# Attention, Fourier mixer and gated mixer on one core: residual additions by accumulating transfers in a rewritten order

## Chip, core and metric

One core of a Trainium2 chip runs the kernel; the other cores are empty. The metric is the device time of one execution in microseconds (us). Below, TensorE is the matrix engine (PE in the profile, PEld its weight loads), VectorE is DVE, ScalarE is ACT, GpSimd is POOL, SyncE is SP. SBUF is the on-chip memory of 128 partitions, PSUM the accumulator memory of eight banks that only TensorE's products, VectorE and ScalarE reach.

## The reference, cut to what matters

```python
# attention: q, k, v are (4 batches, 4 heads, 1088, 32); S1, S2 are (8, 32)
phi(x)  = (x @ S1.T)[..., :, None] * (x @ S2.T)[..., None, :]     # 64 features
kv      = phi(k).T @ v ;  z = phi(k).sum(over the sequence)
x       = (phi(q) @ kv) / (phi(q) @ z + 1e-6)                     # heads joined: (4, 1088, 128)
# first mixture
u       = x + real(fft(fft(x, axis=sequence), axis=channels))
un      = (u - mean(u)) / sqrt(var(u) + 1e-6)
y       = u + relu(un @ w_ch1) @ w_ch2                            # 128 -> 512 -> 128
# second mixture
h       = relu(y @ w_in)                                          # 128 -> 1024
conv    = 3 taps along the sequence, weights per channel
out     = (h * sigmoid(conv)) @ w_out                             # 1024 -> 128
```

All in float32.

## The kernel before

**Layout.** Channels (or features) lie on the 128 partitions and the sequence of 1088 along the free axis. Four batches go through the same stages: `load_attn`, `attn`, `fft`, `moe1`, `moe2`. A batch's sequence is cut into three pieces of 364, 364 and 360 columns (`PIECES`) wherever it goes through PSUM.

**Precision.** A product with plain float32 operands takes two records in the trace. Where speed matters an operand is split into two parts of type float32r, a rounded `hi` and the rest `lo` (`lo_of`: one VectorE operation), and three products replace one: hi·hi, lo·hi, hi·lo. So `z<-yh,win_hi`, `z<-yh,win_lo` and `z<-yl,win_hi` in the trace belong together.

**attn(b)** (lines 309 to 449). `kab_ps` are the two projections of k, `kp` their outer products (VectorE), `kv_ps` the sums over the sequence. In batches 0, 1 and 3 `kv_ps` is transposed by one more product into `kvt_ps`. Four small copies by VectorE then bring it to SBUF: per half of the partitions `kv` (64x64) and `zz` (64x2, `z` in the trace). `den` needs `zz`, `num` needs `kv`. q's features `qa` come in batch 0 from products with repeated weights (`qab_ps`, 128x364); in batches 1 to 3 from small products (`qab_ps`, 128x273), a copy by ScalarE to `qab`, a round trip through DRAM (`qd`) and a product on VectorE. `qab` has a buffer of its own in the pool `at`. The attention output is `x`.

**fft(b)** (from line 452). `xe`, `xo` and `parts` are sums and differences on VectorE; `p_ps` the channel transform, `spec` four sums over the sequence (even and odd frequencies, each an even part `e_ps` and an odd part `o_ps`, 272 columns). For each parity VectorE forms `osb = o_ps - x` and `u = e_ps - osb` for one half of the sequence and `osb = o_ps + x`, `u = e_ps + osb` for the mirrored half, and one column more for the even parity: eight operations of 272 columns and one of one column.

**moe1(b)** (from line 506). ScalarE copies `u` to `uh`, VectorE forms `ul`; products `z` (with `w1`) and `cen` follow, `hid` is the relu. `norm` gives `y`, the reciprocal deviation spread over the partitions. `down(i)` sums `ch` in PSUM, and VectorE multiplies by `y` and adds `u`, both in PSUM; ScalarE copies the result to `yh`, VectorE forms `yl`.

**moe2(b)** (from line 587). Eight chunks of 128 channels: products `z` and relu `h` (ScalarE), middle tap `t` (ScalarE), two outer taps (VectorE, 1087 columns), sigmoid (ScalarE), product with `h` (VectorE), and `acc`, three banks that sum over the chunks.

**Start.** `load64` brings weights as 64-bit words and decodes them with six VectorE operations each 512 columns. `idle` are products of a zero tile `still` with itself whose result nobody reads; 24 of them.

**Buffers.** `slot` gives a tile of the shared wide pool (`mo=12` buffers). PSUM has five banks `mm` and three banks `acc`.

**Order.** Nothing runs as the functions are called: `Program` records 1,956 operations, and `issue` (line 153) sends them in the order of the list `ORDER`, written out as numbers. Every engine's queue is thus a cut of that list, each engine works its own queue in order, and waits follow from the data. In it work of one batch stands between that of the next. All operations are issued by one helper, line 157, which is why the profile puts them on that line; the names of tiles tell them apart. DMAs stand on SP's queue, in the list's order as well; GpSimd issues three loads at the start and makes four broadcasts for batch 0.

Of the kernel before, what the change touches and what calls it, by code (L numbers as in the profile page):

```python
# [19 lines left out]
P = dict(near=(0,), kvt=(0, 1, 3), hs=(), hlo=4, xb=2, sq=(0,), rpe=(0,), up=(0,), mo=12, hid=7, idle=24)  # L20
# [4 lines left out]
D = 128  # L25
# [135 lines left out]
def tile_fwd(ctx, tc, qT, kT, va, srep, mats, thi, tlo, tend, w1, w2, win, cw, wout, out):  # L161
# [73 lines left out]
    if P["idle"]:  # L235

        idle = bank("idle", "acc")
        for i in range(P["idle"]):
            T.matmul(idle[:, :128], still[:, :128], still[:, 128:], start=True, stop=True)
# [494 lines left out]
```

## Time and profile before

| | |
|---|---|
| median of 3 runs | 260.95 us (260.68 to 262.37) |
| profiled execution | 261.13 us |
| its span, first to last instruction | 259.4 us |
| mean granted TensorE clock | 0.993 of full speed |
| instructions | 4622 |
| HBM read, written | 23.27 MB, 3.31 MB |

The profile is of one execution. Matmul records are pipelined and overlap, so an engine that is busy all the time need not be at its peak; what two products cost one behind the other is read from the spacing of their starts, which the chain of waits shows. A granted clock of 1.00 is 2.4 GHz and 0.50 is 1.2 GHz.

### The profile page before, as it was taken

The numbers are of one execution on the slowest core, as the hardware profiler recorded it, in microseconds if no ns is written. First come the engines' busy times: TensorE is split into PE (matmuls) and PEld (weight loads), VectorE is DVE, ScalarE is ACT, GpSimd is POOL, SyncE is SP. The second block draws the span as 40 slices with busy tenths as digits, with TensorE's granted clock in tenths as the row PEclk, the third lists the DMA queues.
The fourth block names the chain that finished last, engine by engine and source line by source line (L and its number), as shares of the span: only waits on it lengthen the run. The fifth ranks groups of instructions, "written<-read, shape, count | busy, mean of one in ns | idle before, by whom it ended". The sixth has DMA issues, their size and how long they took to land.

```text
span 259.4 us, 4622 instructions
## 1 busy us (share of the span) xinstructions
PE 250.8 (97%) x1812; PEld 198.5 (77%) x1812; DVE 234.4 (90%) x356; ACT 183.6 (71%) x330; POOL 6.5 (2%) x15
## 2 busy tenths in 40 slices
PE   7799999999999999999989999999999999999994
PEld 7566679876979887778878877678988877877652
DVE  2588999988999999989999999999999998999970
ACT  3342433972986847873788978996999998999822
POOL 1400000030000000000000000000000000000000
PEclk9799999999999999999999999999999999999999
DMA  7999299385568204184303001500000050000202
GB/s 225 329 402 284 85 304 236 115 228 179 123 147 195 75 24 122 42 175 131 86 4 114 11 0 15 137 0 0 3 0 29 9 143 0 0 3 1 85 0 86
DMA packets 11557, 26.87 MB, mean 104 GB/s; under 512 B 2224, under 2 KB 6832, under 8 KB 11280
## 3 DMA queue, kind: packets, MB, share of 16 engines
q1 hardware_dynamic: 11136, 23.92, 32.9%
q0 software_dynamic: 400, 2.67, 2.9%
q8 instruction: 14, 0.23, 0.4%
q14 instruction: 7, 0.06, 0.1%
HBM read 23.27 MB, written 3.31 MB: 102 GB/s over the span
## 4 chain that ended last, share of the span: by engine, by line
PE 81%; DVE 10%; DMA 4%; ACT 2%; issue 1%; SPq 0%; ACTq 0%; DVEq 0%
PE z L157 25%; PE acc L157 20%; PE ch L157 10%; PE qab_ps L157 5%; DMA q<-qT 4%; PE spec L157 4%; PE kv_ps L157 4%; DVE t L157 4%; PE p_ps L157 3%; PE num L157 3%; PE kab_ps L157 2%; PE cen L157 2%; ACT t L157 1%; PE var L157 1%; DVE ch L157 1%
## 5 line engine op out<-in xcount | busy, mean ns | idle before, releaser
L157 DVE SCALAR_TENSOR_TENSOR t<-h,cw_sb,t 128x1087 f32<-128x1087 f32 x64 | 83.8, 1340 | 0.9 <-ACT t L157 0.4
L157 PE MATMUL acc<-t,wo_sb 128*128 128x364 f32 (+1 forms) x192 | 69.3, 469 | 0.0
L157 ACT ACTIVATE h<-z 128x364 f32<-128x364 f32 (+1 forms) x96 | 41.0, 472 | 15.2 <-PE z L157 14.8
L157 DVE TENSOR_TENSOR t<-t,h 128x1088 f32<-128x1088 f32 (+2 forms) x34 | 40.9, 1217 | 4.6 <-ACT t L157 4.5
L157 PEld LDWEIGHTS acc<-t,wo_sb 128*128 128x128 f32 x192 | 34.3, 189 | 9.1 <-DVE t L157 0.6
L157 ACT ACTIVATE t<-h,cw_sb 128x1088 f32<-128x1088 f32 x32 | 38.4, 1204 | 0.4
L157 ACT ACTIVATE t<-t 128x1088 f32<-128x1088 f32 (+2 forms) x34 | 35.5, 1058 | 4.3 <-DVE t L157 4.3
L157 PE MATMUL z<-yh,win_hi 128*128 128x364 f32 (+1 forms) x96 | 37.2, 414 | 0.0
L157 PE MATMUL z<-yl,win_hi 128*128 128x364 f32 (+1 forms) x96 | 34.1, 366 | 0.2 <-DVE yl L157 0.2
L157 PE MATMUL z<-yh,win_lo 128*128 128x364 f32 (+1 forms) x96 | 34.1, 359 | 0.0
L157 PE MATMUL ch<-hid,w_sb 128*128 128x364 f32 (+1 forms) x96 | 33.3, 469 | 0.0
L157 ACT ACTIVATE hid<-z 128x364 f32<-128x364 f32 (+1 forms) x48 | 21.3, 474 | 7.4 <-PE z L157 7.1
L157 PEld LDWEIGHTS ch<-hid,w_sb 128*128 128x128 f32 x96 | 17.3, 189 | 6.6 <-ACT hid L157 0.5
L157 PEld LDWEIGHTS z<-yh,win_hi 128*128 128x128 f32 x96 | 17.7, 189 | 5.1 <-ACT h L157 1.0
L157 PEld LDWEIGHTS z<-yh,win_lo 128*128 128x128 f32 x96 | 18.1, 189 | 3.1
L157 PEld LDWEIGHTS z<-yl,win_hi 128*128 128x128 f32 x96 | 18.0, 189 | 2.6 <-DVE yl L157 0.5
L157 PE MATMUL z<-uh,w_hi 128*128 128x364 f32 (+1 forms) x48 | 19.2, 410 | 0.0
L157 PE MATMUL z<-uh,w_lo 128*128 128x364 f32 (+1 forms) x48 | 16.9, 358 | 0.0
L157 PE MATMUL z<-ul,w_hi 128*128 128x364 f32 (+1 forms) x48 | 16.4, 359 | 0.0
L157 PE MATMUL p_ps<-mats_sb,parts 128*32 128x128 f32 (+1 forms) x160 | 15.4, 276 | 0.7 <-ACT pe L157 0.7
L157 PEld LDWEIGHTS p_ps<-mats_sb,parts 128*32 128x32 f32 (+1 forms) x160 | 13.2, 142 | 2.2 <-ACT pe L157 0.9
L157 DVE TENSOR_TENSOR kp<-kab_ps,kb 121x512 f32<-121x512 f32 (+1 forms) x24 | 12.2, 546 | 0.5 <-ACT kb L157 0.5
(118 smaller groups left out, 389.3 us busy)
## 6 DMA issues: line engine op xcount, KB each, us to landing
qa<-qd SPq DMA_DIRECT2D x6, 546.0 KB
qb<-qd SPq DMA_DIRECT2D x12, 273.0 KB
v<-va SPq DMA_DIRECT2D x4, 594.0 KB
q<-qT SPq DMA_DIRECT2D x4, 546.0 KB, 6.4
k<-kT SPq DMA_DIRECT2D x4, 544.5 KB
x<-rrd SPq DMA_DIRECT2D x12, 136.5 KB, 4.1
y<-rtd SPq DMA_DIRECT2D x3, 544.0 KB
out<-r SPq DMA_DIRECT2D x8, 182.0 KB
```

The source lines that it names most:

```text
L157: fn(*args, **kw)
```

## The change

- `idle`: 36 products instead of 24; `still` has 128 columns and is both operands.
- `kva`: in batches 0 and 1 ScalarE makes the four copies to `kv` and `zz`.
- `ua`: in batches 1 to 3 ScalarE copies `o_ps` to `osb` and the one column to `u`; VectorE forms `u = e_ps ∓ osb` (four operations of 272 columns); then one transfer issued by GpSimd, from SBUF to SBUF, adds `x` onto `u` (128x1088).
- `ca`: in batch 2 VectorE writes `ch * y` over `y` in SBUF, and per piece a transfer issued by GpSimd adds `u` onto it; `yh` and `yl` are made from there.
- `qab` takes a slot of the wide pool.
- `load64` writes the decoded value into its place one operation earlier; the operations are as many.
- `dm`, `dl`, `ea` and `hs` are empty in this kernel, so what hangs on them isn't built.
- `ORDER` is new: 1,965 numbers, all positions changed. In the new list 17 idle products stand ahead of TensorE's first product on q (13 before); the load of q for batch 2 stands ahead of the transfers of `qd`; and TensorE's queue has, between the last `spec` product of a batch and the first product on its `uh`, in batch 1 17 z, 8 acc and 7 kab products (16 z and 4 acc before), in batch 2 33 and 9 (7 and 4), in batch 3 26 and 9 (15 and 4), z counted in records of three to a product and acc in products. Between the last `ch` product of a piece of batch 2 and the first z on its `yh` stand 6.5, 7.2 and 5.8 us of products for the first, middle and last piece by the durations of the trace.

```diff
-P = dict(near=(0,), kvt=(0, 1, 3), hs=(), hlo=4, xb=2, sq=(0,), rpe=(0,), up=(0,), mo=12, hid=7, idle=24)
+P = dict(near=(0,), kvt=(0, 1, 3), hs=(), hlo=4, xb=2, sq=(0,), rpe=(0,), up=(0,), mo=12, hid=7, dm=(), dl=(), late=2, kva=(0, 1), ua=(1, 2, 3), ca=(2,), ea=(), idle=36)
...
-            V.scalar_tensor_tensor(ei, hi, -(1 << 30), ei, op0=ALU.bitwise_and, op1=ALU.bitwise_or)
-            V.tensor_scalar(mi, ei, -(1 << 23), None, op0=ALU.bitwise_and)
+            x = use(o, w, e)
+            xi = x.bitcast(I32)
+            V.scalar_tensor_tensor(xi, hi, -(1 << 30), ei, op0=ALU.bitwise_and, op1=ALU.bitwise_or)
+            V.tensor_scalar(mi, xi, -(1 << 23), None, op0=ALU.bitwise_and)
...
-    still = cst.tile([128, 256], F32, name="still")
+    still = cst.tile([128, 128], F32, name="still")
...
-            T.matmul(idle[:, :128], still[:, :128], still[:, 128:], start=True, stop=True)
+            T.matmul(idle[:, :128], still, still, start=True, stop=True)
...
-            qab = at.tile([128, SP // 2], F32, tag="qab", name=f"qab{b}")
+            qab = slot(f"qab{b}")[:, :SP // 2]
...
-            V.tensor_copy(kv[r, :, 32 * h2:32 * h2 + 32], kvv[h2][:, :, 0:32])
-            V.tensor_copy(zz[r, DJ - 1 + DJ * h2:DJ + DJ * h2 + ZW + 2 * DJ:ZW + 2 * DJ], kvv[h2][:, :, 32])
+            copy = A.copy if b in P["kva"] else V.tensor_copy
+            copy(kv[r, :, 32 * h2:32 * h2 + 32], kvv[h2][:, :, 0:32])
+            copy(zz[r, DJ - 1 + DJ * h2:DJ + DJ * h2 + ZW + 2 * DJ:ZW + 2 * DJ], kvv[h2][:, :, 32])
...
+            if b in P["ua"]:
+                if not par:
+                    A.copy(u[:, 0:1], e_ps[:, 272:273])
+                osb = ff.tile([128, 272], F32, tag="osb", name=f"osb{b}_{par}", bufs=2)
+                A.copy(osb, o_ps[:, :272])
+                V.tensor_tensor(u[:, here], e_ps[:, :272], osb, op=ALU.subtract)
+                V.tensor_tensor(u[:, back], e_ps[:, :n], osb[:, :n], op=ALU.add)
+                if not par:
+                    G.dma_start(u, x[:, :SEQ], accum_op=ALU.add)
+                continue
...
-            V.tensor_tensor(c[:, :w], c[:, :w], y[:, o:o + w], op=ALU.mult)
-            V.tensor_tensor(c[:, :w], c[:, :w], u[:, o:o + w], op=ALU.add)
-            A.copy(yh[:, o:o + w], c[:, :w])
-            lo_of(V, yl[:, o:o + w], c[:, :w], yh[:, o:o + w])
+            if b in P["ca"]:
+                s = y[:, o:o + w]
+                V.tensor_tensor(s, c[:, :w], s, op=ALU.mult)
+                G.dma_start(s, u[:, o:o + w], accum_op=ALU.add)
+            else:
+                s = c[:, :w]
+                V.tensor_tensor(s, s, y[:, o:o + w], op=ALU.mult)
+                V.tensor_tensor(s, s, u[:, o:o + w], op=ALU.add)
+            A.copy(yh[:, o:o + w], s)
+            lo_of(V, yl[:, o:o + w], s, yh[:, o:o + w])
```

## Rows read from the trace of the kernel before

**Rows 1.** The page's first part: busy us, share of the span, instructions of each engine.

```profile
PE 250.8 (97%) x1812; PEld 198.5 (77%) x1812; DVE 234.4 (90%) x356; ACT 183.6 (71%) x330; POOL 6.5 (2%) x15
```

**Rows 2.** Chain of waits by line: 58 to 102, 102 to 180, 180 to 240 us.

```profile
by line: DVE t L157 21.9%; PE z L157 12.2%; PE kv_ps L157 7.6%; ACT t L157 6.4%; issue 5.6%; DVE ch L157 5.1%; PE num L157 4.3%; DVE x L157 3.2%; DVE parts L157 3.2%; DVE qa L157 2.9%; DVE ul L157 2.7%; DVE u L157 2.5%; DVE yl L157 2.2%; PE
...
by line: PE z L157 35.8%; PE acc L157 19.5%; PE ch L157 19.0%; PE p_ps L157 6.1%; PE num L157 4.6%; PE spec L157 4.5%; PE kv_ps L157 3.2%; PE cen L157 2.0%; PE var L157 1.6%; PE den L157 1.4%; ACT t L157 1.4%; ACT pe L157 0.8%; ACT sq L157 
...
by line: PE z L157 41.8%; PE acc L157 36.4%; PE ch L157 12.2%; PE spec L157 5.9%; PE cen L157 1.7%; PE p_ps L157 1.5%; PE var L157 1.0%
```

**Rows 3.** Windows: us, busy of PE, PEld, DVE, ACT, POOL, clock, DMA share, GB/s.

```profile
8.40:11.80 3.40, 3.40 (x11) 2.32 (x11) 1.94 (x6) 1.17 (x3) 2.69 (x6) 0.50 0.97 352
...
58.00:102.00 44.00, 43.85 (x365) 36.76 (x364) 42.53 (x70) 28.99 (x51) 0.99 (x3) 1.00 0.50 128
...
102.00:180.00 78.00, 77.27 (x587) 61.36 (x585) 74.50 (x100) 62.92 (x109) 0.00 (x0) 1.00 0.24 60
...
180.00:240.00 60.00, 60.00 (x318) 48.16 (x316) 58.49 (x60) 55.91 (x91) 0.00 (x0) 1.00 0.08 21
```

**Rows 4.** Pieces of the chain of waits in order of time: start, us, what, records.

```profile
22.87 1.09 PE idle L157 x8
...
194.87 0.61 PE acc L157 x2
...
196.31 0.50 PE z L157 x3
...
242.24 13.69 PE acc L157 x44
```

**Rows 5.** Timeline of PE, 0 to 16 us: start, us, instruction, idle before it.

```profile
1.17 4.97 PE L157 MATMUL idle<-still 128*128 128x128 f32 x26 [1.17 <-DVE still L157]
...
8.17 2.55 PE L157 MATMUL qab_ps<-q,sq_sb 128*128 128x364 f32 x4 [2.03 <-DMA q<-qT]
...
12.15 1.44 PE L157 MATMUL qab_ps<-q,sq_sb 128*128 128x364 f32 x4
```

**Rows 6.** Waits of PE, 20 to 240 us: total, times, longest.

```profile
PE qab_ps L157 <- DMA q<-qT: 0.6, 1, 0.6
```

**Rows 7.** VectorE's groups by shape: busy us, mean ns of one, idle before.

```profile
L157 DVE TENSOR_TENSOR osb_AluOpType.add<-spec,x 128x272 f32<-128x272 f32 x4 | 1.7, 436 | 0.1
...
L157 DVE TENSOR_TENSOR u<-spec,x 128x1 f32<-128x1 f32 x4 | 0.6, 146 | 0.0
...
L157 DVE TENSOR_TENSOR ch<-ch,u 128x364 f32<-128x364 f32 x8 | 4.3, 540 | 0.2
...
L157 DVE COPY kv<-kvt_ps 64x64 f32<-64x64 f32 x6 | 1.3, 217 | 0.1
...
L157 DVE COPY z<-kvt_ps 64x2 f32<-64x2 f32 x6 | 1.0, 159 | 1.2 <-PE kvt_ps L157 1.2
```

**Rows 8.** ScalarE's groups by shape, the same columns.

```profile
L157 ACT COPY qab<-qab_ps 128x273 f32<-128x273 f32 x6 | 2.2, 390 | 4.6 <-PE qab_ps L157 4.6
...
L157 ACT COPY vk<-kv_ps 33x128 f32<-33x128 f32 x6 | 1.5, 257 | 3.3 <-PE kv_ps L157 3.3
...
L157 ACT CAST uh<-u 128x1088 fp32r<-128x1088 f32 x3 | 3.3, 1104 | 1.1 <-DVE u L157 1.1
```

**Rows 9.** Timeline of POOL at the start.

```profile
10.88 0.55 POOL L157 DMA_DIRECT2D tab_end<-tend  x1
```

**Rows 10.** DMA issues: count, KB each, median us from issue to landing.

```profile
q<-qT SPq DMA_DIRECT2D x4, 546.0 KB, 6.4
...
tab_hi<-thi POOLq DMA_DIRECT2D x1, 1096.0 KB, 8.9
...
out<-r SPq DMA_DIRECT2D x4, 180.0 KB, 4.0
...
tab_end<-tend POOLq DMA_DIRECT2D x1, 411.0 KB, 13.9
...
rtd<-rt SPq DMA_DIRECT2D x3, 34.0 KB, 1.5
```

More of the change, by code (lines that the diff above doesn't have):

```diff
@@ L195, in load64 @@
             V.tensor_scalar(ei, ei, 3, 0x3FFFFFF8, op0=ALU.logical_shift_left, op1=ALU.bitwise_and)
-            V.scalar_tensor_tensor(ei, hi, -(1 << 30), ei, op0=ALU.bitwise_and, op1=ALU.bitwise_or)
-            V.tensor_scalar(mi, ei, -(1 << 23), None, op0=ALU.bitwise_and)
+            x = use(o, w, e)
+            xi = x.bitcast(I32)
+            V.scalar_tensor_tensor(xi, hi, -(1 << 30), ei, op0=ALU.bitwise_and, op1=ALU.bitwise_or)
+            V.tensor_scalar(mi, xi, -(1 << 23), None, op0=ALU.bitwise_and)
             V.scalar_tensor_tensor(m, low, 2.0 ** -52, m, op0=ALU.mult, op1=ALU.mult)
-            V.tensor_tensor(use(o, w, e), e, m, op=ALU.add)
+            if src.tensor.name in P["ea"]:
+                G.dma_start(x, m, accum_op=ALU.add)
+            else:
+                V.tensor_tensor(x, x, m, op=ALU.add)
             then(o, w, e)
@@ L266, in tile_fwd @@
     w2_sb = cst.tile([D, 4, D], F32, name="w2_sb")
-    w2_hi = cst.tile([D, 4, D], F32R, name="w2_hi")
-    w2_lo = cst.tile([D, 4, D], F32R, name="w2_lo")
     win_hi = cst.tile([D, DFF], F32R, name="win_hi")
@@ L272, in tile_fwd @@
     wo_sb = cst.tile([D, NFC, D], F32, name="wo_sb")
+    if P["dl"]:
+        wo_hi, nwo_hi, nwo_lo = (cst.tile([D, NFC, D], F32R, name=n) for n in ("wo_hi", "nwo_hi", "nwo_lo"))
+    if P["hs"]:
+        w2_hi, w2_lo = (cst.tile([D, 4, D], F32R, name=n) for n in ("w2_hi", "w2_lo"))
     def consts_fft():
@@ L305, in consts_moe2, with both @@
         load64(cw, 3 * NFC, plain(cw_sb.rearrange("p c k -> p (c k)")))
-        load64(wout, DFF, plain(wo_sb.rearrange("p c d -> p (c d)")))
+        def both(o, w, x):
+            hi, nhi, nlo, w = (t.rearrange("p c d -> p (c d)")[:, o:o + w] for t in (wo_hi, nwo_hi, nwo_lo, wo_sb))
+            A.copy(hi, w)
+            A.activation(nhi, w, AF.Copy, scale=-1.0)
+            V.scalar_tensor_tensor(nlo, w, -1.0, nhi.bitcast(F32), op0=ALU.mult, op1=ALU.subtract)
+        load64(wout, DFF, plain(wo_sb.rearrange("p c d -> p (c d)")), both if P["dl"] else lambda o, w, x: None)
     def attn(b):
@@ L542, in down @@
                     T.matmul(c[:, :w], l[:, f], r, start=(f == 0 and m == 0), stop=(f == 3 and m == len(hid[i, f]) - 1))
-            V.tensor_tensor(c[:, :w], c[:, :w], y[:, o:o + w], op=ALU.mult)
-            V.tensor_tensor(c[:, :w], c[:, :w], u[:, o:o + w], op=ALU.add)
-            A.copy(yh[:, o:o + w], c[:, :w])
-            lo_of(V, yl[:, o:o + w], c[:, :w], yh[:, o:o + w])
+            if b in P["ca"]:
+                s = y[:, o:o + w]
+                V.tensor_tensor(s, c[:, :w], s, op=ALU.mult)
+                G.dma_start(s, u[:, o:o + w], accum_op=ALU.add)
+            else:
+                s = c[:, :w]
[3 more added lines that the diff above has]
+            lo_of(V, yl[:, o:o + w], s, yh[:, o:o + w])
         def norm():
@@ L589, in moe2 @@
         acc = [bank(f"acc{b}_{i}", "acc") for i in range(3)]
-        hs, ts = {}, {}
+        hs, ts, ns = {}, {}, {}
         def up(f):
@@ L604, in taps @@
             for k, d, s in ((0, t[:, 1:], h[:, :SEQ - 1]), (2, t[:, :SEQ - 1], h[:, 1:])):
+                if k == 0 and NFC * b + f in P["dm"]:
+                    left = slot(f"s{b}_{f}")[:, :SEQ - 1]
+                    A.activation(left, s, AF.Copy, scale=cw_sb[:, f, k:k + 1])
+                    G.dma_start(d, left, accum_op=ALU.add)
+                    continue
                 V.scalar_tensor_tensor(d, s, cw_sb[:, f, k:k + 1], d, op0=ALU.mult, op1=ALU.add)
@@ L611, in gate, with rest @@
                 V.tensor_tensor(t, t, h, op=ALU.mult)
+            if NFC * b + f in P["dl"]:
+                nh = ns[f] = mo.tile([128, WIDE], F32R, tag="wide", name=f"n{b}_{f}")[:, :SEQ]
+                A.activation(nh, ts[f], AF.Copy, scale=-1.0)
         def down(f):
             for i, (o, w) in enumerate(PIECES):
-                T.matmul(acc[i][:, :w], wo_sb[:, f], ts[f][:, o:o + w], start=(f == 0), stop=(f == NFC - 1))
-        for f in range(NFC + 3):
+                terms = ((nwo_hi, ns[f]), (nwo_lo, ns[f])) if f in ns else ((wo_sb, ts[f]),)
+                for m, (l, r) in enumerate(terms):
+                    T.matmul(
+                        acc[i][:, :w],
+                        l[:, f],
+                        r[:, o:o + w],
+                        start=(f == 0 and m == 0),
+                        stop=(f == NFC - 1 and not any(NFC * b + g in P["dl"] for g in range(NFC - P["late"], NFC))),
+                    )
+            if f in ns:
+                G.dma_start(ns[f], ts[f], accum_op=ALU.add)
+        def rest(f):
+            later = any(NFC * b + g in P["dl"] for g in range(f + 1, NFC))
+            for i, (o, w) in enumerate(PIECES):
+                T.matmul(acc[i][:, :w], wo_hi[:, f], ns[f][:, o:o + w], start=False, stop=(f >= NFC - P["late"] and not later))
+        for f in range(NFC + 3 + P["late"]):
             if f < NFC:
@@ L623, in moe2 @@
                 gate(f - 2)
-            if f >= 3:
+            if 3 <= f <= NFC + 2:
                 down(f - 3)
+            if f - 3 - P["late"] in ns:
+                rest(f - 3 - P["late"])
         for i, (o, w) in enumerate(PIECES):
```

148 rows, old and new, of the table ORDER are left out of this document.

## The prediction

> **What bounds the kernel now.** I read the page first: TensorE is busy for 97% of the span, VectorE for 90%, ScalarE for 71%, GpSimd for 2% [rows 1]. Two engines that are both nearly full have to be told apart by stretch, so I took the chain of waits in three stretches [rows 2]. From 58 to 102 us VectorE holds most of it: the taps (DVE t) alone 21.9%, and with ch, x, parts, qa, ul, u and yl the listed rows add up to 43.7%, all of VectorE to about half. From 102 to 180 us nearly everything is TensorE, and from 180 to 240 us all of it. The windows of the same stretches show VectorE at 42.5 of 44, 74.5 of 78 and 58.5 of 60 us [rows 3]: close behind TensorE all along, but not ahead of it after 102 us.
>
> A busy TensorE could still be one that waits inside its products, so I compare with its pieces on the chain: two records of an acc product take 0.61 us and three z records 0.50 us [rows 4]. These are the spacings of products that follow each other with nothing between. The end of the chain is 44 acc records in 13.69 us, 0.31 each: that spacing, without a hole [rows 4]. TensorE's listed shares add up to all of the 60 us from 180 to 240, and to 97.7% of the 78 us before, which leaves 1.8 us there [rows 2]. So after 102 us a faster VectorE has little to give; what can be won lies before.
>
> At the start TensorE runs idle products for 4.97 us, stands still for 2.03 us until q has landed, and then runs its first four records of qab in 2.55 us, where the next four take 1.44 us [rows 5]. The window behind it has a granted clock of 0.50 from 8.4 to 11.8 us, which is 1.2 GHz; in the stretches later it is 1.00 [rows 3].
>
> **The change part by part.** All sums are against the profiled execution: its own time is 261.13 us, its span 259.4, so 1.7 us lie around the span; the median of the runs is 260.95, 0.2 below.
>
> *Idle products.* Before, 13 of the 24 stand at the head of TensorE's queue; in the new list 17 of 36 do. The 13 end at 6.14 us. Four more at the full clock, at most 0.27 us each (the eight idle records in 1.09 us are four products [rows 4]), end near 7.2 us, still before q lands at about 8.1: they cost nothing. What they may bring is the clock: TensorE stands still for about 1 us instead of 2. If the clock stays at 2.4 GHz from 8.4 to 11.8 us, the 3.4 us of work there [rows 3] take 1.7, and the chain stands on TensorE there. Bounds 0 and -1.7; I take -1.7, because the stretch at 0.50 follows the only hole of TensorE that is longer than a microsecond, and that hole is halved. The Trainium skill, page "TensorE: Matmul & The Clock Gate", section "What's actually happening", says that the throttled state is the default, that work releases it, and that the number of slow products at the start differs from run to run of one kernel; by that the 1.7 us would come in some runs only, and the sum would be 1.7 higher in the others. The rows here are of one execution and can't show that.
>
> The other 8 added products stand between work of the first two batches. On a dense TensorE they cost 8 x 0.27 = 2.2 us [rows 4], in holes nothing. Bounds 0 and +2.2; I take half, +1.1.
>
> *Order of the transfers.* Q of batch 2 is issued in the old list behind a qd transfer on SP's queue, and TensorE waits 0.6 us for it [rows 6]. In the new list it stands before qd. -0.6 (0 to -0.6). The new list also moves k, v, cw and the broadcasts of the denominators past each other on SP; I cost that at nothing, since no other wait of TensorE for a transfer is in the answer of [rows 6].
>
> *Key-value copies by ScalarE, batches 0 and 1.* Per batch VectorE loses two copies of 0.217 and two of 0.159 us [rows 7]: 0.75, so 1.5 in all. ScalarE takes eight copies of at most 0.257 (its 33x128 copy [rows 8]): +2.1 at most. In batch 0 the z copy sits in the chain to den, where VectorE is full of weight decoding and ScalarE is not: -0.3 (0 to -0.6). Batch 1's copies lie inside 58 to 102 us.
>
> *Attention output onto the spectra by a transfer, batches 1 to 3.* Per batch VectorE did four osb of 0.436, four u of the same shape and one column of 0.146 [rows 7]: 3.6 us. Four u remain, 1.75. VectorE is rid of 1.85 us a batch, 5.6 in all. ScalarE gets two copies of 272 columns at 0.390 and one column at under 0.257 [rows 8], about 1.0 a batch, 3.0 in all. GpSimd gets one issue (0.55 us [rows 9]) a batch, with nothing queued behind it.
>
> *First mixture's residual, batch 2.* Three additions of 0.540 leave VectorE [rows 7], 1.6 us; three issues go to GpSimd. ScalarE's copy yh and VectorE's yl now wait for the landing.
>
> VectorE's sum: 1.5 + 5.6 + 1.6 = 8.7 us less. What of it reaches the end? Within 58 to 102 us 1.85 + 0.75 = 2.6 us are removed, half of the chain there is VectorE's: -1.3 (0 to -2.6). Between 102 and 180 us the chain is off TensorE for 1.8 us, with 5.4 us of VectorE's relief about: I take all of it, -1.8 (0 to -1.8). After 180 us: 0, TensorE has no hole. ScalarE's added 5 us lie where it is busy for 29.0 of 44 and 62.9 of 78 us [rows 3] and are hidden; only batch 3's last microsecond falls near 180 us, where it has 55.9 of 60, and would cost at most itself.
>
> *The added waits.* From the last spectrum product to the first product on uh the chain is osb 0.39, two u 0.87, the issue 0.55, the landing T, and uh 1.10 [rows 7 to 9]: 2.9 + T. In the new list TensorE has between these two products, in batch 1, 17 z records and 8 acc products (2.8 + 4.9 = 7.7 us, and 7 small kab products, so near 9); in batch 2, 33 and 9 (5.5 + 5.5 = 11.0); in batch 3, 26 and 9 (4.3 + 5.5 = 9.8), by the spacings of [rows 4]. So T may be about 6 us in batch 1, 8 and 7 in the others. No row shows an accumulating transfer, or one from SBUF to SBUF. The bounds of T: 1.5 (34 KB) and 13.9 (411 KB, queued behind two others on the same queue) [rows 10]. The nearest by size is q, 546 KB in 6.4 us while the start's transfers were all in flight; by queue it is tab_hi, 1,096 KB in 8.9 us. I take 5.5 us: it is covered, 0. The waiting instruction is uh on ScalarE: behind it stand the relu copies that free the five mm banks of PSUM, so TensorE can go on only until its banks are full.
>
> For the three pieces of batch 2 the chain is the product with y 0.54, issue 0.55, landing (a 180 KB store takes 4.0 [rows 10]) and yh about 0.5 (by the 0.390 of 273 columns [rows 8]): 5.6 us. TensorE has 6.5, 7.2 and 5.8 us of work between the first, middle and last piece's ch products and the first z on it. That is tight, and in the list the copy of the middle piece stands right behind its own transfer on ScalarE, with a sigmoid, pe and ph behind it. +0.6 (0 to +4).
>
> *The rest.* still's fill is shorter, but q sets the start; qab takes a slot of the shared wide pool of 12, so three more tiles go round it: 0 (up to one evicted tile's wait, some 1.3 us). The decode of the weights has the same instructions. dm, dl, ea and hs are empty.
>
> Sum: -1.7 + 1.1 - 0.6 - 0.3 - 1.3 - 1.8 + 0.6 = -4.0, from 261.1 to 257.1. The median stood 0.2 below the profiled execution, so I say 257.0.
>
> **The rivals.** *TensorE is the bound throughout.* VectorE's relief becomes idle time of VectorE, and the eight idle products cost in full: 261.1 - 1.7 - 0.6 + 2.2 = 261.0, or 259.4 if half of the products fall in holes and half a microsecond of VectorE's time counts. For it: no hole from 180 us on. Against it: the chain of 58 to 102 us.
>
> *VectorE is the bound throughout*, and all 8.7 us come off: 252.4. The windows have it at 95 to 97% [rows 3], and it seldom waits. Against it: the chain is not on it after 102 us. The Trainium skill, page "Perfetto Trace Analysis", section "Identifying the Most-Contended Engine", speaks for this one: there a busy share of products says little and the weight loads' share counts; here that is 77% [rows 1], below VectorE's 90%. The spacing of the products is what I hold against it.
>
> *The transfers land late* (the other side). An accumulating transfer has to read both u and x; if it takes the 8.9 us of tab_hi [rows 10], the chain is 11.8 us against covers of 9, 11 and 9.8: 2.8 + 0.8 + 2.0 = 5.6 us of standing still, while ScalarE is held at uh with relu copies behind it. With the pieces at +0.6 and none of VectorE's gains: 261.1 - 1.7 + 1.1 - 0.6 - 0.3 + 5.6 + 0.6 = 265.8. It decides from T of about 6 us on, where batch 1's cover ends; at 7 us it would be some 1 us.
>
> *The clock still falls at the start*, all else as forecast: 258.7.
>
> **How the numbers follow.** The forecast has 0.46, TensorE-bound 0.21, late transfers 0.16, clock still falling 0.10, VectorE-bound 0.07. A measurement of this kernel can tell about 1%, 2.6 us: faster means below 258.3, slower above 263.6. The forecast's own range is 254.8 to 259.3; nine tenths of its chance count as faster (0.41), with the VectorE case (0.07) and a third of the clock case (0.03): 0.51. Slower: most of the late transfers, 0.15, and 0.01 of the rest: 0.16. The rest, 0.33, is within 1%. The range for 8 in 10 goes from 252.5, near the VectorE case, to 263.5, half-way into the late transfers.
>
> **What would show it.** Right: a granted clock of 1.00 in the first windows after q has landed; u<-x transfers that land within about 6 us of issue; no long idle time of TensorE in front of z on uh; VectorE's busy time near 226 us; acc records without holes to the end. Wrong: ScalarE waiting several microseconds at uh or yh with TensorE idle behind it; a clock of 0.50 after 8 us; or VectorE's time falling by 8.7 us with the span unchanged.

## The result and the profile after

| | before | after |
|---|---|---|
| median (all runs so far, 4 each) | 261.25 us | 264.3 us (263.76 to 265.34) |
| ratio of the two | | 1.0111 (95% interval 1.0072 to 1.0151) |
| profiled execution, its span | 261.13, 259.4 us | 264.83, 263.1 us |
| mean granted clock | 0.993 | 1.000 |

The forecast was 257.0 us; the kernel became 1.1% slower, beyond the range's upper end of 263.5. Here and below a ratio leaves out executions that took over 1.5% longer than the fastest of the same kernel.

The page's first part after, against [rows 1]:

```profile
PE 255.4 (97%) x1836; PEld 201.2 (76%) x1836; DVE 228.2 (87%) x330; ACT 187.4 (71%) x347; POOL 11.2 (4%) x21
```

VectorE did get rid of its work: 234.4 to 228.2 us busy. Its records overlap a little; the durations of the groups that the change touches (copies, `osb`, `u`, `ch`) fall by the 8.7 us that were forecast, those of all VectorE records by 8.5. TensorE is busy for 4.6 us longer, though its useful products are the same.

The windows after (columns as in [rows 3]):

```profile
8.40:11.80 3.40, 3.06 (x21) 2.34 (x20) 1.28 (x6) 1.18 (x4) 0.69 (x2) 1.00 1.04 422
58.00:102.00 44.00, 42.72 (x354) 35.19 (x353) 38.55 (x56) 29.74 (x54) 0.92 (x1) 1.00 0.55 144
102.00:180.00 78.00, 76.92 (x578) 60.54 (x577) 69.13 (x90) 59.68 (x107) 3.44 (x4) 1.00 0.31 72
180.00:240.00 60.00, 59.97 (x317) 47.93 (x316) 57.12 (x56) 56.17 (x96) 0.85 (x1) 1.00 0.13 30
```

The clock at the start is 1.00. VectorE's relief is visible as its idle time, 4 us in 58 to 102 and 5.4 in 102 to 180; TensorE did not become denser by it.

The start and the place of batch 1's transfer after: two rows of TensorE's timeline (as [rows 5]), pieces of the chain of waits (as [rows 4]), and the landings (as [rows 10]):

```profile
1.04 6.18 PE L157 MATMUL idle<-still 128*128 128x128 f32 x34 [1.04 <-DVE still L157]
7.06 0.78 PE L157 MATMUL qab_ps<-q,sq_sb 128*128 128x364 f32 x2
```

```profile
91.61 0.60 PE acc L157 x2
...
93.33 6.58 DMA u<-x
...
100.01 1.11 ACT uh L157
...
101.16 0.96 PE z L157 x4
```

```profile
u<-x POOLq DMA_DIRECT2D x3, 544.0 KB, 4.7
...
y<-u POOLq DMA_DIRECT2D x2, 182.0 KB, 2.9
```

The hole ahead of q is gone; the first product on q also starts earlier, at 7.06 us instead of 8.17. Batch 1's `u<-x` took 6.58 us and uh waited for it; TensorE stood still for 1.0 us ahead of `z<-uh`.

To see where time goes when both engines look full, I counted TensorE's progress: each record adds a constant of its kind, taken from spacings (z 0.165, acc and ch 0.303, spec 0.122 us and so on, idle products 0), so that both kernels come to the same 229.3 us. The table gives the time at which so much is done. Its times are my estimate, good to some 0.3 us, as far as another choice of the constants moves them; small steps between neighbours are differences of mixture, not waits. e17 and e18 are the last two experiments.

| useful work done (us) | before | after | e17 | e18 |
|---|---|---|---|---|
| 16 | 29.1 | 27.1 | 27.3 | 27.7 |
| 64 | 84.6 | 83.0 | 83.0 | 83.5 |
| 72 | 92.7 | 92.2 | 92.2 | 92.6 |
| 80 | 100.8 | 101.6 | 101.5 | 100.7 |
| 128 | 151.5 | 152.1 | 152.0 | 151.3 |
| 136 | 160.4 | 162.4 | 161.1 | 160.4 |
| 152 | 176.9 | 179.7 | 177.3 | 176.6 |
| 216 | 242.4 | 245.8 | 243.3 | 242.7 |
| end of TensorE | 255.9 | 259.6 | 257.1 | 256.5 |

After is ahead by 2.0 us, keeps 1.6 until 83 us, and has lost 2.4 by 102; then it loses 1.4 from 152 to 162 and 0.8 from 162 to 180.

### The profile page after: what moved, and what is told of

Its sections match the earlier page's. It is cut to its first block, busy times and chain, and to the rows that moved or that the text cites. A ratio compares the mean times of both kernels' runs of the same rounds, so it can differ in the third digit from the quotient of the medians.

```text
span 263.1 us, 4687 instructions
## 1 busy us (share of the span) xinstructions
PE 255.4 (97%) x1836; PEld 201.2 (76%) x1836; DVE 228.2 (87%) x330; ACT 187.4 (71%) x347; POOL 11.2 (4%) x21
## 4 chain that ended last, share of the span: by engine, by line
PE 59%; DVE 21%; DMA 13%; ACT 4%; issue 2%; SPq 0%; ACTq 0%; POOLq 0%; DVEq 0%
PE z L157 16%; DVE t L157 15%; PE acc L157 10%; PE ch L157 6%; PE spec L157 5%; PE p_ps L157 5%; DMA u<-x 4%; PE kv_ps L157 4%; DMA v<-va 4%; PE qab_ps L157 3%; PE num L157 3%; DMA y<-rtd 2%; PE kab_ps L157 2%; DVE em L157 2%; PE den L157 1%
## 5 line engine op out<-in xcount | busy, mean ns | idle before, releaser
L157 ACT ACTIVATE h<-z 128x364 f32<-128x364 f32 (+1 forms) x96 | 41.8, 475 | 11.2 <-PE z L157 10.9
L157 PE MATMUL z<-yl,win_hi 128*128 128x364 f32 (+1 forms) x96 | 33.5, 368 | 0.0
L157 PE MATMUL z<-yh,win_lo 128*128 128x364 f32 (+1 forms) x96 | 32.3, 353 | 0.0
L157 PE MATMUL z<-uh,w_hi 128*128 128x364 f32 (+1 forms) x48 | 18.5, 410 | 1.1 <-ACT uh L157 1.0
L157 PE MATMUL z<-uh,w_lo 128*128 128x364 f32 (+1 forms) x48 | 16.3, 346 | 0.0
```

The lines of the kernel that those rows point to most:

```text
L157: fn(*args, **kw)
```

## The experiments

Theory L: the transfers onto u put their landing on TensorE's path. Theory O: the rewritten order is the worse one, by itself. Theory V: VectorE's time decides. Ratios are to the kernel before on the same chip; after stands at 1.0111. The experiments ran on several chips, on which the kernel before takes 261.2 to 262.2 us in the median.

**All additions onto u back on VectorE.**

```diff
-                    G.dma_start(u, x[:, :SEQ], accum_op=ALU.add)
+                    V.tensor_tensor(u, u, x[:, :SEQ], op=ALU.add)
```

> The changed kernel, but the three transfers of x onto u are VectorE additions of 1088 columns (about 1.3 us each) at the same places of the order. Theory L (the landing of u<-x stands on TensorE's path: in the changed kernel it took 6.6 us in batch 1 and 4.7 in the others, and TensorE lost some 2.4 us between 83 and 102 us): the wait of uh falls from 7.5 to about 1.4 us behind the last u, and 2 to 3 us come back: 261.5 to 262.5. Theory O (the rewritten order itself is the worse one, the transfers are hidden): no gain, 264 to 266, since VectorE has 3.9 us more to do. Theory V (VectorE's time decides): 266 to 268.

Measured: 264.4 us, 1.012 (1.0073 to 1.0166): no gain. L in its strong form falls; 1.4 us came back by 101 us and went again in batches 2 and 3, 0.7 of it in a wait of TensorE for VectorE's `ul` at 200 us that after doesn't have.

**The pieces of batch 2 back on VectorE.**

```diff
-ca=(2,)
+ca=()
```

> The changed kernel, but batch 2's residual is added by VectorE in PSUM again (three operations of 0.54 us in place of three transfers), same order. If the pieces' transfers (landings of 2.9 to 3.0 us) cost what TensorE lost from 165 to 190 us: 263.2, 1.1 less than the changed kernel. If they are covered: 264.3, or up to 1.6 more from VectorE's three operations. Theory L and theory O say the same here.

Measured: 266.0 us, 1.0185 (1.0136 to 1.0235): 1.7 us worse. The window from 165 to 180 us, first after, then this run, and this run's longest wait of PE in it:

```profile
165.00:180.00 15.00, 14.32 (x89) 11.10 (x88) 11.93 (x14) 10.86 (x19) 2.56 (x3) 1.00 0.35 69
```

```profile
165.00:180.00 15.00, 12.94 (x76) 9.62 (x75) 13.47 (x17) 9.83 (x17) 0.00 (x0) 1.00 0.14 35
```

```profile
PE z L155 <- DVE pe L155: 1.4, 1, 1.4
```

With three additions more on VectorE, TensorE waits 1.4 us there for a VectorE operation. So the pieces' transfers are no loss; the new order, written for them, needs them.

**Both edits**, so that no accumulating transfer is left.

> Both edits: no accumulating transfer is left, all additions are VectorE's, the order is the changed kernel's. Theory L: the two gains add up, 260.5 to 261.5, as fast as the kernel before or a little faster, since the 1.7 us won at the start are kept. Theory O: 263.5 to 266, the loss stays because it is the order's. Theory V: 268 or more.

Measured: 266.2 us, 1.0196 (1.0135 to 1.0256), a little over the upper end that O had. TensorE's two longest waits in it are for VectorE:

```profile
PE z L155 <- DVE pe L155: 1.4, 1, 1.4
PE z L155 <- DVE ul L155: 0.7, 1, 0.7
```

After has neither wait. So 2.1 of the 4.9 us are the price of putting the additions back into an order that was written without them. The other 2.8 us stand without any accumulating transfer: for them O fits. This run alone doesn't separate the two.

**Four idle products more in the kernel before**, behind the thirteenth.

```diff
-idle=24
+idle=28
```

> The kernel before with four idle products more, all behind the thirteenth at the head of TensorE's queue; nothing else is changed. If the hole of 2.0 us ahead of the first product on q is what brings the clock to 0.50, it is about 1 us now, the clock stays at 1.00 from 8.4 to 11.8 us and 1.5 to 1.9 us come off: 259.3 of 261.2. If the hole doesn't decide, or TensorE's gain is lost to VectorE later (its bound): 261.0 to 261.3.

Measured: 261.8 us, 1.0027 (0.9989 to 1.0064): no gain. The rows of PE's and VectorE's timelines:

```profile
7.62 1.46 PE L155 MATMUL qab_ps<-q,sq_sb 128*128 128x364 f32 x4 [0.69 <-POOL tab_hi L155]
```

```profile
19.83 0.89 DVE L155 TENSOR_SCALAR em<-em 128x512 f32<-128x512 f32 x2 [2.09 <-ACT em L155]
```

The clock stayed at 1.00 and the lead was 1.7 us at 17 us; VectorE then waited 2.09 us in the decode, and at 40 us 0.3 was left. But this can't be put down to the four products. In two later runs with the old start and its 13 idle products (e7 and e8 below) the clock is 1.00 there as well; their first products on q:

```profile
7.67 1.46 PE L155 MATMUL qab_ps<-q,sq_sb 128*128 128x364 f32 x4 [0.58 <-ACT sq_sb L155]
```

```profile
7.64 1.46 PE L155 MATMUL qab_ps<-q,sq_sb 128*128 128x364 f32 x4 [1.70 <-ACT sq_sb L155]
```

In these runs and in e4 q landed 4.9 to 5.0 us behind its issue; in the profiled execution of the kernel before it took 6.39, and that made its start late. The run with a hole of 1.70 us kept a clock of 1.00, so the hole of 2.03 us isn't shown to be what brought it to 0.50. Of the 96 executions of the kernel before during these runs, 46 had a mean clock of 1.000 (median 261.5 us), and all 96 have a median of 261.8. The profiled execution, at 0.993, had a rare start: 17 of the 96 had 0.993 or lower (median 263.7), the other 79 took 261.5.

**Only the 17 idle products at the head.**

```diff
-idle=36
+idle=17
```

> The changed kernel with 17 idle products, those at the head of TensorE's queue; the 19 others (0.27 us each on a full TensorE, 5.1 us together, 2.2 of them the eight that the change adds) are left out, the order is otherwise the same. Theory I (they stand in TensorE's way): 259 to 261. Theory H (they stand in holes in which TensorE would wait for VectorE anyway): 263.5 to 264.5. If they keep the clock at 2.4 GHz, windows with a clock of 0.50 appear and it is slower, 265 or more.

Measured: 268.8 us, 1.0251 (1.0195 to 1.0306). The same window in this run and after:

```profile
28.00:38.00 10.00, 9.39 (x45) 5.85 (x45) 6.58 (x15) 2.47 (x8) 0.00 (x0) 0.56 0.57 183
```

```profile
28.00:38.00 10.00, 9.84 (x100) 7.91 (x98) 9.71 (x21) 4.05 (x11) 0.00 (x0) 1.00 0.83 248
```

The products between the work keep the clock at 1.00 here; without them it fell to 0.50 from 29.1 to 39.4 us (the expectation of e12 below puts that too early), 0.56 on average in this window. TensorE just ahead of the fall, and in the stretch at 0.50:

```profile
24.00:29.10 5.10, 4.36 (x38) 2.91 (x34) 4.02 (x10) 3.12 (x9) 0.00 (x0) 1.00 0.53 173
29.10:39.40 10.30, 9.76 (x43) 6.45 (x44) 6.81 (x15) 1.59 (x6) 0.00 (x0) 0.50 0.60 162
```

Its longest single wait since 8 us was 0.9 us, so this fall didn't follow a long hole either. What the 19 products cost where they stand can't be read from this run; the eight latest are priced below.

**Only batch 1's addition on VectorE.**

```diff
-                    G.dma_start(u, x[:, :SEQ], accum_op=ALU.add)
+                    if b == 1:
+                        V.tensor_tensor(u, u, x[:, :SEQ], op=ALU.add)
+                    else:
+                        G.dma_start(u, x[:, :SEQ], accum_op=ALU.add)
```

> The changed kernel, but x is added onto u by VectorE in batch 1 alone; batches 2 and 3 keep their transfers. Batch 1's transfer landed 6.6 us behind its issue, and TensorE stood 1.2 us ahead of the first product on uh; in the run with all three by VectorE that stretch was 1.4 us shorter at 102 us, and the gain was lost in batches 2 and 3. If that is so, both gains stay: 262.5 to 263.2. If the 1.4 us are eaten by whatever binds later: 264.3.

Measured: 264.0 us where the kernel before took 262.2, 1.0058 (1.0035 to 1.0082), against 1.0111 (1.0072 to 1.0151); the two intervals overlap a little, and the last experiment repeats the step on one chip. L holds for batch 1 alone. In the profiles of the eight other experiments with this transfer in the new order it landed in 5.4 to 7.2 us; batches 2 and 3 mostly in 4.6 to 4.9. At 5.6 (e13) TensorE had no wait for uh, at 7.2 (e12) one of 1.6 us. In the five profiles with such a wait (after, e2, e12, e16, e17) it is the landing less 5.53 to 5.54 us: that much is covered in this order.

**The copies by ScalarE alone, in the kernel before.**

```diff
-            V.tensor_copy(kv[...], ...)
+            copy = A.copy if b in (0, 1) else V.tensor_copy
+            copy(kv[...], ...)
```

> The kernel before, with the key-value copies of batches 0 and 1 by ScalarE and nothing else. The prediction took -0.3 (0 to -0.6) for batch 0 and a part of -1.3 for batch 1: 260.5 to 260.9. If VectorE's relief doesn't reach the end in the old order: 261.2. If ScalarE's queue is late there: 261.5 to 263.

Measured: 0.9999 (0.9955 to 1.0042), inconclusive: neither -0.3 nor zero can be told apart.

**The transfers onto u in the old order**, each new operation at the place of the one that it replaces.

```diff
+            if b in (1, 2, 3):
+                ...
+                A.copy(osb, o_ps[:, :272])
+                ...
+                    G.dma_start(u, x[:, :SEQ], accum_op=ALU.add)
```

> The kernel before with the accumulating transfers of u in batches 1 to 3 (osb by ScalarE, four u by VectorE, then the transfer), in the old order, which has work of some 5.1, 3.6 and 4.9 us between the last spectrum product and the first on uh. With the landings seen in the changed kernel (6.6, 4.7, 4.7 us) and 3.3 us for osb, u, the issue and uh, TensorE would stand still for about 4.8, 4.4 and 3.0 us: 270 to 274, and then the new order was needed for the transfers and repays most of them. If the transfers are no burden: 259.5 to 261, and the order alone is the loss.

Measured: 285.9 us, 1.0868 (1.0823 to 1.0914). Waits of ACT and PE (total, times, longest):

```profile
ACT uh L155 <- DMA u<-x: 18.2, 3, 7.4
```

```profile
PE z L155 <- ACT h L155: 11.5, 2, 6.7
PE cen L155 <- ACT h L155: 5.6, 1, 5.6
```

This is well over the 270 to 274 expected. The transfers need the new order, or another with such cover: ScalarE is held at uh, TensorE runs out of banks behind it and stops for 6.7, 5.6 and 4.9 us, longer than landing less cover (4.8, 4.4 and 3.0), since it waits for relus that stand behind uh on ScalarE. Within each stop the granted clock falls to 0.50, at 100.1, 161.6 and 216.2 us, and stays there for 6.8 us (0.964 in the mean).

**The new order for the front, the old one for the rest**, with the old residual additions, but ScalarE's copies and qab in the wide pool: 555, 765 and 340 operations. Where an operation of the old rest would have found no free bank or buffer, it was put off until one was.

```diff
-ORDER = before
+ORDER = after[:555] + [i for i in before if i not in after[:555]]
```

> The arithmetic of the kernel before (all residual additions by VectorE), with the key-value copies by ScalarE and qab in the wide pool; the first 555 operations (to about 62 us) in the new order with its 33 idle products, all others in the order of the kernel before. Theory S (the lead of 1.9 us is won in the new order's start, and the new order's later part loses it and more): the lead is kept and 259.0 to 259.8 comes out of 261.2. Theory B (the old order's later part is bound by VectorE and gives any lead back, as it did in the run with four idle products more): 260.8 to 262.

> The same with the first 765 operations (to about 84 us, just ahead of batch 1's spectra) in the new order with all 36 idle products, the rest old. Theory S: the lead was still 1.6 us at 83 us in the changed kernel, so 259.3 to 260.2. If the loss begins ahead of 84 us, in the order: 261 to 262. Theory B: 261 to 262 as well, but then the run to 62 us shows no gain either.

> The same with the first 340 operations (to about 42 us) in the new order with 31 idle products. Theory S: the lead at 40 us was 1.9 us, so 259 to 259.8, the same as to 62 us. Theory B: 261 to 262.

Measured: 1.0059 (1.0034 to 1.0085), 1.0065 (1.0042 to 1.0088), 1.0036 (1.0003 to 1.0068). Theory S falls, and theory B's times are missed too, since all three are slower than the kernel before. e11 was ahead of it by 1.9 us at 99 us, level at 135 and behind by 1.9 at 170. Its longest waits of VectorE and TensorE in the last of these stretches:

```profile
DVE ch L155 <- DMA y<-rtd: 2.0, 1, 2.0
```

```profile
PE ch L155 <- ACT hid L155: 1.5, 1, 1.5
```

Before, that wait for y was 0.4 us. `rtd<-rt`, the transfer ahead of y, was followed by y's issue after 3.3 us here and after 1.6 before; why is not shown. A lead brought into an order can thus be lost at a transfer of that order. Of the other half, from 99 to 135 us, 1.4 us went in three waits of 0.4 to 0.6 us. VectorE was not shown as the cause, and a seam of two orders may lose what neither loses by itself.

**Eight idle products fewer after**, the latest left out.

```diff
-idle=36
+idle=28
```

> The changed kernel without its eight latest idle products (those from about 28 us to 72 us; 2.2 us on a full TensorE). With 17 left in all the clock fell to 0.50 in the windows from 20 to 30 us and it was 4.5 us slower than the changed kernel; here those up to 28 us stay. If they stand in TensorE's way (theory I): 262 to 263. If they lie in holes (theory H): 264.0 to 264.6. If these too hold the clock: a clock under 1.00 somewhere from 28 to 75 us and 265 or more.

Measured: 264.9 us, 1.0128 (1.0075 to 1.0181), with a clock of 1.00 throughout: these eight cost nothing that shows, and they aren't needed for the clock.

**Neighbours.** The rows of num and var behind batch 2's sums, after:

```profile
153.97 2.05 PE L157 MATMUL num<-qa,kv 128*64 128x364 f32 x10
155.94 0.55 PE L157 MATMUL var<-sq,one_v 128*32 128x68 f32 x12
156.42 0.82 PE L157 MATMUL num<-qa,kv 128*64 128x364 f32 x2
157.18 0.67 PE L157 MATMUL var<-sq,one_v 128*32 128x68 f32 x20
157.78 0.43 PE L157 MATMUL z<-yh,win_hi 128*128 128x364 f32 x1
```

```diff
 num3_1[0:64]
+num3_1[64:128]
-var2 rows 64:96, 96:128, 64:96, 96:128, ...
-num3_1[64:128]
-var2 rows 0:32, 32:64, 0:32, ...
+var2 rows 64:96, 96:128, 0:32, 32:64, and again
```

> The changed kernel, but in TensorE's queue num3_1's second half (64 output rows) stands directly behind its first, and the 32 var products of batch 2 (32 output rows each) stand in fours again; the new order had put 10 var products between the halves and ran the var in twos. In the changed kernel this stretch of num and var took 3.8 us, in the kernel before, where halves and fours are neighbours, 2.6. Theory P (neighbours on different rows of the output run side by side, so the order prices the product): 263.1, 1.2 less. If TensorE has slack there: 264.3.

```profile
153.00 2.06 PE L155 MATMUL num<-qa,kv 128*64 128x364 f32 x12
154.98 0.68 PE L155 MATMUL var<-sq,one_v 128*32 128x68 f32 x32
155.59 0.43 PE L155 MATMUL z<-yh,win_hi 128*128 128x364 f32 x1
```

Measured: 263.5 us, 1.006 (1.0017 to 1.0103), against 264.2 for the changed kernel with other buffers of qab on the same chip (e16 below); the stretch takes 2.6 us instead of 3.8. By the starts of single records, those of two halves next to each other come 0.01 us apart and the next pair 0.30 later; a half that stands alone takes 0.30 to 0.40. TensorE was busy either way: no view of waits shows this loss.

The new order has done the same to q's products for batch 3, which no experiment touched. Four records, two halves of 64 rows, stand together before (first fence) and in two places after (second):

```profile
76.31 0.63 PE L157 MATMUL qab_ps<-q,sab_sb 128*64 128x273 f32 x4
76.87 0.44 PE L157 MATMUL kv_ps<-v,kp 121*128 121x66 f32 x2
```

```profile
83.75 0.67 PE L157 MATMUL qab_ps<-q,sab_sb 128*64 128x273 f32 x2
84.36 0.27 PE L157 MATMUL den<-qa,z 128*32 128x91 f32 x1
...
84.79 0.67 PE L157 MATMUL qab_ps<-q,sab_sb 128*64 128x273 f32 x2
85.39 0.41 PE L157 MATMUL p_ps<-mats_sb,parts 128*32 128x128 f32 x4
```

By the starts they take 0.61 and 0.60 us after and 0.56 together before. That is 0.65 of the 1.1 us that after loses between 83 and 92 us in the table.

**More cover for batch 1's transfer, by moving two num pairs ahead; and both edits of order.**

```diff
+num2_1[0:64], num2_1[64:128], num2_0[0:64], num2_0[64:128], relu h0_7
 uh1 = u1
 z on uh1
 ...
-num2_1, num2_0 between cen and var
```

> The changed kernel, all transfers kept, but two num pairs of batch 2 (1.3 us of TensorE) and one relu are put ahead of the first products on uh in batch 1. Theory L (the landing of batch 1's transfer lacks 1.2 to 1.5 us of cover): the stop in front of z on uh goes, 262.9 to 263.3, like the run with that addition by VectorE. If what binds later eats it: 264.3.

> Both edits of order. If the two are separate losses of TensorE's time, they add up: 261.7 to 262.1, equal to the kernel before within what can be measured. If VectorE or ScalarE bind behind them: 263 or more.

Measured: 266.5 us, 1.0184 (1.0121 to 1.0247), and 265.4 us, 1.0139 (1.0076 to 1.0202); both are slower than expected. PE's timeline of the first:

```profile
102.81 0.43 PE L155 MATMUL z<-uh,w_hi 128*128 128x360 f32 x1 [0.40 <-ACT hid L155]
...
104.14 0.43 PE L155 MATMUL cen<-uh,cen_r 128*128 128x364 f32 x1 [0.40 <-ACT hid L155]
...
106.46 0.44 PE L155 MATMUL cen<-uh,cen_r 128*128 128x360 f32 x1 [0.56 <-ACT sq L155]
...
107.62 0.67 PE L155 MATMUL var<-sq,one_v 128*32 128x68 f32 x28 [0.32 <-ACT sq L155]
```

The stop at uh is gone and 1.7 us of stops stand behind it, where the num products had covered ScalarE's hid and sq. Work moved is not work gained. Pairs again give about 1.1 us on top (266.5 to 265.4).

**qab in two buffers of its own.**

```diff
-            qab = slot(f"qab{b}")[:, :SP // 2]
+            qab = at.tile([128, SP // 2], F32, tag="qab", name=f"qab{b}", bufs=2)
```

> The changed kernel with qab in two buffers of its own instead of slots of the wide pool, same order. The prediction took 0, up to 1.3 us for one evicted tile's wait. If the three tiles cost nothing: 264.3; if the wide pool is what holds the later stretches: 262 to 263.5.

Measured: 264.2 us, 1.0101 (1.0071 to 1.0131): the wide pool is not the cause.

**The copy pe behind its products.** After, TensorE's row of small products ends like this:

```profile
175.38 1.07 PE L157 MATMUL p_ps<-mats_sb,parts 128*32 128x128 f32 x22
177.13 0.41 PE L157 MATMUL p_ps<-mats_sb,parts 128*32 128x128 f32 x2 [0.68 <-ACT pe L157]
```

```diff
-pe3 = p_ps3_2[0:64]
 p_ps3_2[64:96, 3]
+pe3 = p_ps3_2[0:64]
```

> The changed kernel with num3 and var in their groups as in the run on pairs, and one move more: ScalarE's copy pe of batch 3 stands behind the last of the 24 small p_ps products, where the new order had put it one product ahead, so that TensorE waited 0.7 us for the copy (0.95 us between two starts, against 0.10 to 0.20 elsewhere in the row). If both are TensorE's own losses: 264.3 - 1.2 - 0.8 = 262.3. If the second is hidden: 263.1.

```profile
174.01 1.07 PE L155 MATMUL p_ps<-mats_sb,parts 128*32 128x128 f32 x24
175.01 0.43 PE L155 MATMUL z<-yh,win_hi 128*128 128x364 f32 x1
```

Measured: 262.1 us, 1.0015 (0.9998 to 1.0031).

> The same, and x is added onto u by VectorE in batch 1. Its transfer landed 5.4 to 7.2 us behind its issue in the runs so far and stopped TensorE for 0 to 1.6 us. If the three losses add up: 264.3 - 1.2 - 0.8 - 1.2 = 261.1, level with the kernel before (261.2 to 262.2 on these chips, so a ratio of 1.000, 0.997 to 1.003). If another wait takes their place: 262.3 or more, a ratio of 1.004 or more.

Measured: 261.3 us, 0.9992 (0.9975 to 1.0009). On the same chip that is 0.8 us less than e17, in 12 executions each. The three edits together take back the whole of the change's loss, 3.0 us where 3.2 were expected. This is the best version found; it does not beat the kernel before. That kernel has the same fault of pe, in batch 2 (one wait of 0.7 us); mending it there was not tried, nor was putting qab's halves together again.

## Why the prediction was wrong

The step that failed is "What of it reaches the end?": VectorE's relief was entered with -1.3 and -1.8 us, and the new order with no price of its own. In their place the runs show a relief that brings no net gain (e18, with 7.2 us less work on VectorE than the kernel before by the durations of its records, takes the same time), and an order that costs TensorE 1.2 us at num and var and 1.1 us between 83 and 92 us. That the waits for u and the clock were mis-sized too comes on top.

- *VectorE's relief (-3.1).* The 8.7 us came off VectorE, but the windows give them back as its idle time. With relief left in (the copies, u of batches 2 and 3, the pieces) and two of the order's faults mended, e18 only draws level. The relief is not worthless: taking the pieces' part back costs 1.7 us in the new order. It pays for that order and doesn't come on top. What is argued and not shown is that nothing of it is left: e18 still carries the loss of 1.1 us between 83 and 92 us, so a gain of that size could hide behind it. VectorE's share of the chain in one order gave no price for it in another.
- *The order's own price (0 in the sum).* I counted in TensorE's list only what lies between the last spec and the first product on uh. Num and var apart cost 1.2 us (3.8 against 2.6). The stop at pe, 0.7 us, is no loss against the kernel before, which has its like in batch 2; mending it is a gain that offsets another loss. That other loss is the stretch from 83 to 92 us, 1.1 us in the table, still there in e17 and e18. By the rows above, 0.65 of it are the halves of qab torn apart; the rest, where small products of two batches alternate in TensorE's list, stays open. Neither was tried by itself.
- *The waits for u (0, with T at 5.5).* The mechanism was right, and the threshold nearly: cover ends at 5.5 us instead of about 6, and "at 7 us it would be some 1 us" is 1.6 at 7.2. T measured 4.7 in two batches and 5.4 to 7.2 in batch 1, where transfers of x and qb are issued while it is under way; that these slow it is not shown. The term was +1.0 in the profiled execution (6.58 us) and 0.2 to 0.5% by the ratios (e17 to e18, after to e6), 0.6 to 1.4 us.
- *The pieces (+0.6).* Covered: landings of 2.9 to 3.0 us. No cost.
- *The clock (-1.7).* The window has 1.00, as forecast, but not for the reason given: the old start has it too when q lands in 5 us, with the hole at 0.58 or 1.70 us. And the gain was one of the profiled execution and its like: 79 of 96 executions of the kernel before had a mean clock above 0.993. The 17 others took some 2 us longer, the seven among them with just 0.993 some 1.4, so the size was about right for these, though the profiled one, at 261.13 us, was no slower than the rest. In the new order with its products between the work, 2 of 79 executions had 0.993 or lower; the medians don't show that. The Trainium skill, "TensorE: Matmul & The Clock Gate", section "What's actually happening", says that the number of slow products at the start varies from run to run of one kernel. The mean clocks of the 96 executions, 0.979 to 1.000, agree, and the sentence with the sum 1.7 us higher was the one to follow.
- *The eight idle products (+1.1).* Nothing, as far as e12 shows for the eight latest; the 19 between the work hold the clock, which e5 shows and the prediction didn't see.
- *q ahead of qd (-0.6), the copies (-0.3).* No wait of TensorE for q is left after; neither could be priced alone.

Of the rivals, late transfers came nearest in time (265.8), and in batch 1 in kind, though not as the whole. VectorE as the bound throughout (252.4) is excluded: 8.7 us came off it and the time rose, and e18 with most of that off takes the time of the kernel before.

## What to carry to other kernels

A rewritten order is a change of its own: before pricing what it carries, go through each engine's new queue for pairs of small products torn apart, for copies put between the products that they read, and for the cover of every new wait. Before time taken from the second busiest engine is entered as a gain, name the stop of the busiest one that it ends. And a row of one execution, such as a late load or a clock at the start, is a gain only if the other executions have it too.

## What was not expected of the hardware

- Products with 64 output rows on different halves run side by side if they are neighbours in the queue (records of two in 0.31 us, of one in 0.30 to 0.40), and so do var's 32-row products (0.06 us for four, and as much for two where they stand in twos).
- The same accumulating transfer of 544 KB within SBUF took 4.6 to 4.9 us mostly, and 5.4 to 7.2 in batch 1, where others were in flight; 182 KB took 2.9.
- Without idle products between the work the clock fell well after the start (e5, 0.50 from 29.1 to 39.4 us), without a wait of TensorE over 0.9 us ahead of it; with a hole of 1.70 us at the start it stayed at 1.00 (e8).
